# Score and PV matmuls on 128 rows instead of 64, with the low half of K stored twice

## The chip, the cores and the metric

The kernel runs on one core of one Trainium2 chip. The metric is device time in microseconds (us), the median of the runs that were timed; lower is better. The profiled execution is a single run with its own time, which is given beside its span.

## The reference

Attention over 4 batches of 8 heads (576 positions, 64 wide) feeds a maximum of three matrix products and a projection (called first and second layer here), and that feeds a routed mixture of 8 experts. Cut to what matters:

```python
q_rot, k_rot = rotate(q), rotate(k)                      # rotary embedding, (4, 8, 576, 64)
scores = (1 / np.sqrt(D)) * np.matmul(q_rot, k_rot.transpose(0, 1, 3, 2))
attn = np.exp(scores - scores.max(-1, keepdims=True))
attn = attn / (attn.sum(-1, keepdims=True) + 1e-09)
x = np.matmul(attn, v).transpose(0, 2, 1, 3).reshape(2304, 512)
h = np.maximum(np.maximum(x @ w1, x @ w2), x @ w3)       # 512 -> 768
x = h @ w_out                                            # 768 -> 512
# then: each token goes to the expert of its largest gate logit, relu(x @ w1[e]) @ w2[e]
```

## The kernel before

**Precision.** Most float32 products are made from pairs of float16: an operand is split into a high part and a low part (what the high part leaves over), and high*high, high*low and low*high are summed in PSUM. Batch 0 of the attention computes its scores in float32 instead, on 64 rows (lines 651 and 652); its PV products go the float16 way like all the others.

**Units.** The attention is a list of 36 units a batch, 144 in all, numbered from 0 through the batches: 32 units of 128 query rows by one head, and 4 tail units that hold the last 64 query rows of two heads. A unit goes through these steps, each on its own engine:

- scores on PE, in batches 1 to 3: `qt` holds Q transposed, 128 rows a head, of which 64 rows are Q's high part and 64 its low part. `kh` holds K's high part transposed and stored twice, on rows 0 to 63 and again on 64 to 127, so that one 128-row matmul gives high*high plus low*high (lines 659 and 660: 512 and 64 columns). K's low part `kl` is stored once; of two heads that share a block, one lies on rows 0 to 63 and the other on 64 to 127. Its product uses the 64 rows of `qt` with Q's high part (lines 661 and 662). Tail units do the same for two heads, each into 64 columns of the array (lines 671 to 674).
- DVE scales the scores and takes the row minimum (L677), ACT takes the exponential (L679) and its float16 high part (L681), DVE the low part (L686).
- the queue of SP transposes both into `pt` by a DMA of 9 blocks of 128 x 128 (L689).
- PV on PE: 13 matmuls on 128 rows (L713, L714, L716), and a last one on 64 rows (L717), which multiplies `pt` block 4 with the low part of V's last 64 positions.

**K and Q preparation.** Batches 1 to 3 have two halves of 4 heads each. For a half: load K and Q; a sum of squares of both gives the scales (its matmul is line 100, "the stats matmul" below); POOL and DVE apply the rotary embedding to K and then to Q (`rope_of`, lines 411 to 435; the products with the sine go into a buffer `t2`, of which there is one); ACT writes K's high part twice (L472), DVE its low part (L475, three instructions of 640, 512 and 128 elements a row); ACT and DVE split Q (L483, L486); SP transposes `khs` (18 blocks, L503), `qs` (18 blocks, L504) and `kls` (10 blocks, L505) into one tile `kq`, of which three exist. The second half of a batch is first read by the fifth unit of that batch (units 40, 76 and 112).

**Order.** Python records the instructions with priorities, and a scheduler that simulates the engines fixes each engine's order at build time. At run time every engine goes through its own list in order and waits where a semaphore tells it to. Between the units PE does first-layer (L817 to L819) and second-layer matmuls (L865 to L867) of earlier batches, which read `self.w`. The expert part begins when the attention and both layers are done, at about 660 us of the span.

## Time and profile before

| | us |
|---|---|
| median of 3 runs | 954.32 (945.73 to 957.39) |
| profiled execution, its own time | 952.98 |
| span of the profiled execution | 951.1 |
| PE busy | 830.7 (87%) |
| DVE busy | 670.7 (71%) |
| ACT busy | 574.8 (60%) |
| POOL busy | 240.5 (25%) |

The busy time of PE counts matmuls that overlap as one stretch, and a matmul's record is longer than the time until the next may start; so what a matmul costs PE is read from the starts of matmuls that follow each other. Times in the profile are counted from the start of the span.

### The profile page before, as it was taken

The page shows a single profiled execution, that of the slowest core. Times are in us where ns is not written, and L with a number is a line of the kernel's source. Part 1 is how long each engine was busy: PE and PEld are TensorE (multiplying, and loading weights), DVE is VectorE, ACT ScalarE, POOL GpSimd, SP SyncE. Part 2 cuts the span into 40 slices and gives each one's busy share as a digit, 9 for nine tenths or more (in the row PEclk, how much of TensorE's full clock was granted, in tenths as well). Part 3 has the DMA queues.
Part 4 walks back from the last instruction along what each step waited for, and adds up shares of the span by engine and source line. Part 5 has one row for each costly group of instructions (what it writes and reads, how often), then busy time and mean ns, then how long its engine had stood idle before and what let it go on. Part 6 is the DMA issues. An engine that isn't in the chain of part 4 may idle for free. (4 is left out here: it accounts for less than half of the span.)

```text
span 951.1 us, 18856 instructions
## 1 busy us (share of the span) xinstructions
PE 830.7 (87%) x7304; PEld 653.7 (69%) x7304; DVE 670.7 (71%) x1350; ACT 574.8 (60%) x1001; POOL 240.5 (25%) x232
## 2 busy tenths in 40 slices
PE   3578998779799878699989899899499999998995
PEld 2345775567576656468667577588498889997994
DVE  6997889987487787486566666534557777766771
ACT  3767888666476566475465546421545777776772
POOL 8460002421030432020030100001431644434320
PEclk9555567989799999799979999799799999999999
DMA  8698788795898897897658865720511111133110
GB/s 244 168 198 197 174 160 178 151 190 103 112 173 146 134 180 101 122 153 144 70 112 141 121 107 97 88 41 24 200 46 34 38 42 56 45 133 123 42 45 20
DMA packets 264502, 110.66 MB, mean 116 GB/s; under 512 B 240175, under 2 KB 256703, under 8 KB 263888
## 3 DMA queue, kind: packets, MB, share of 16 engines
q1 hardware_dynamic: 254848, 79.82, 48.9%
q0 software_dynamic: 9552, 29.51, 9.4%
q8 instruction: 61, 1.00, 0.6%
q14 instruction: 41, 0.34, 0.2%
HBM read 74.97 MB, written 9.80 MB: 89 GB/s over the span
## 5 line engine op out<-in xcount | busy, mean ns | idle before, releaser
L817 PE MATMUL mm<-xT,w 128*128 128x256 f16 (+1 forms) x792 | 196.8, 263 | 2.0 <-DVE h L833 0.9
L818 PE MATMUL mm<-xT,w 128*128 128x256 f16 (+1 forms) x792 | 196.6, 263 | 0.0
L819 PE MATMUL mm<-xT,w 128*128 128x256 f16 (+1 forms) x792 | 196.2, 263 | 0.0
L679 ACT ACTIVATE p<-s,bi 128x576 f32<-128x576 f32 x144 | 106.0, 736 | 96.0 <-DVE s L677 74.3
L686 DVE SCALAR_TENSOR_TENSOR p<-p,p 128x576 f16<-128x576 f32 x144 | 128.7, 899 | 15.5 <-ACT p L681 15.0
L677 DVE TENSOR_SCALAR_CACHE_REDUCE s<-s,qk_sc 128x576 f32<-128x576 f32 x108 | 88.0, 821 | 61.9 <-PE s L662 51.7
L713 PE MATMUL o<-v,pt 128*128 128x64 f16 (+1 forms) x576 | 63.4, 207 | 48.8 <-DMA pt<-p 46.5
L1127 ACT CAST h<-r 128x512 fp32r<-128x512 f32 x80 | 93.4, 1205 | 19.0 <-DMA r<-moe_w,widx 12.9
L681 ACT ACTIVATE p<-p 128x576 f16<-128x576 f32 x144 | 97.0, 680 | 4.7 <-DMA pt<-p 2.6
L1128 DVE TENSOR_TENSOR l<-r,h 128x512 fp32r<-128x512 f32 x80 | 89.8, 1162 | 5.1 <-ACT h L1127 4.6
L817 PEld LDWEIGHTS <-w 128*128 128x128 f16 x792 | 80.6, 102 | 17.2 <-issue 8.7
L819 PEld LDWEIGHTS <-w 128*128 128x128 f16 x792 | 80.8, 102 | 11.7 <-issue 4.1
L713 PEld LDWEIGHTS <-pt 128*128 128x128 f16 x576 | 48.0, 105 | 59.2 <-DMA pt<-p 51.4
L818 PEld LDWEIGHTS <-w 128*128 128x128 f16 x792 | 80.9, 102 | 10.7 <-issue 3.8
L1218 PE MATMUL pa<-xh,h 128*128 128x256 f32 x288 | 81.7, 286 | 0.8 <-ACT xh L1149 0.8
L1219 PE MATMUL pa<-xl,h 128*128 128x256 f32 x288 | 81.9, 285 | 0.2 <-DVE xl L1150 0.2
L1220 PE MATMUL pa<-xh,l 128*128 128x256 f32 x288 | 81.8, 285 | 0.0
L833 DVE SCALAR_TENSOR_TENSOR hm<-mm,winv,hm 128x512 f32<-128x512 f32 (+1 forms) x60 | 40.1, 668 | 39.3 <-PE mm L819 37.5
L651 PE MATMUL s<-kq 64*128 64x512 f32 (+1 forms) x72 | 56.9, 970 | 8.9 <-ACT p L679 8.9
L865 PE MATMUL mm<-oh,h 128*128 128x256 f16 (+1 forms) x216 | 60.4, 282 | 4.5 <-DVE hm L833 4.3
L714 PE MATMUL o<-v,pt 128*128 128x64 f16 (+1 forms) x576 | 62.7, 207 | 1.1 <-DVE v L619 1.1
L1190 PE MATMUL pb<-h,hl 128*128 128x512 f32 x152 | 60.8, 403 | 3.0 <-DVE hl L1222 2.8
(308 smaller groups left out, 2082.7 us busy)
## 6 DMA issues: line engine op xcount, KB each, us to landing
wr<-moe_w POOLq DMA_DIRECT2D x10, 768.0 KB
yscr<-y SPq DMA_DIRECT2D x18, 257.0 KB, 4.0
rk<-k SPq DMA_DIRECT2D x8, 512.0 KB, 4.3
vraw<-v SPq DMA_DIRECT2D x8, 512.0 KB, 4.6
rq<-q SPq DMA_DIRECT2D x7, 512.0 KB, 5.0
wr<-moe_w_out POOLq DMA_DIRECT2D x4, 768.0 KB
pt<-p SPq DMA_TRANSPOSE x144, 3.3
v<-v SPq DMA_DIRECT2D x16, 128.0 KB, 7.7
```

Source lines behind the costliest of these rows:

```text
L677: nc.vector.tensor_scalar(out=sf, in0=sf, scalar1=sc, scalar2=None, op0=ALU.mult, op1=ALU.min, accum_out=bi)
L679: nc.scalar.activation(p32, sf, AF.Exp, bias=bi, scale=-1.0, accum_out=st["sum", c][:, h:h + 1])
L681: nc.scalar.activation(p16[:, 0], p32, AF.Copy, scale=32768.0)
L686: nc.vector.scalar_tensor_tensor(out=p16[:, 1], in0=p32, scalar=32768.0, in1=p16[:, 0], op0=ALU.mult, op1=ALU.subtract)
L713: nc.tensor.matmul(out, lhsT=pt[:, blk], rhs=sel(vh, blk), start=blk == 0, stop=False)
L817: nc.tensor.matmul(pv[:, i], lhsT=wh, rhs=xT[:, k, :n], start=k == 0, stop=False)
L818: nc.tensor.matmul(pv[:, i], lhsT=wh, rhs=xT[:, 4 + k, :n], start=False, stop=False)
L819: nc.tensor.matmul(pv[:, i], lhsT=wl, rhs=xT[:, k, :n], start=False, stop=k == 3)
L1127: nc.scalar.copy(T["h1"][:, :, j], r[:, :, j])
L1128: nc.vector.tensor_tensor(out=T["l1"][:, :, j], in0=r[:, :, j], in1=T["h1"][:, :, j].bitcast(F32), op=ALU.subtract)
L1219: nc.tensor.matmul(ps[:, i], lhsT=h1[:, k, j + i], rhs=xl[:, k], start=False, stop=False)
L1220: nc.tensor.matmul(ps[:, i], lhsT=l1[:, k, j + i], rhs=xh[:, k], start=False, stop=k == 3)
```

## The change

In batches 1 to 3 the low part of K is laid out like the high part: all 18 blocks, stored twice (on rows 0 to 63 and on 64 to 127). The low score matmuls then take the same 128-row `qt` block as the high ones, which adds the product low*low. The last PV matmul takes all 128 rows of `pt` block 4; rows 64 to 127 of the V operand are zeros. The tail units issue their eight matmuls in another order: both heads' 512-column ones, both heads' 64-column ones, first with `kh`, then with `kl`.

What comes with it: `kls` grows from 10 to 18 blocks and takes the slot of `t2`, so the rope of Q, which needs `t2`, waits until the transposes have read `kls`; the transposes of K become a step of their own, ahead of the rope of Q. DVE makes `kls` in one instruction and POOL copies it to the second place. POOL zeroes 64 rows of each V tile. The tile `kq` grows from 48 to 54 blocks, and room for it is made by putting the tail output `xt32` into a part of `self.w` that is no longer used by then. A switch that was off (`PE_LO`) is removed with its code.

```diff
@@ split_k
-            kls = self.raws.tile([P, 10, P], F16, tag="kls", name="kls", bufs=1)
+            kls = self.raws.tile([P, 18, 2, D], F16, tag="t2", name="kls", bufs=1)
             nc.scalar.activation(khs, rot.unsqueeze(2).to_broadcast([P, 18, 2, D]), AF.Copy, scale=s)
-            for sl, d0, out in ((slice(8, 18), D, kls[:, 0:10, D:2 * D]), (slice(0, 8), 0, kls[:, 0:8, 0:D]),
-                                (slice(16, 18), 0, kls[:, 8:10, 0:D])):
-                nc.vector.scalar_tensor_tensor(out=out, in0=rot[:, sl], scalar=s, in1=khs[:, sl, 0],
-                                               op0=ALU.mult, op1=ALU.subtract)
+            nc.vector.scalar_tensor_tensor(out=kls[:, :, 0], in0=rot, scalar=s, in1=khs[:, :, 0],
+                                           op0=ALU.mult, op1=ALU.subtract)
+            nc.gpsimd.tensor_copy(kls[:, :, 1], kls[:, :, 0])
@@ tr
-            kq = self.att.tile([P, 48, P], F16, tag=f"kq{(2 * b + hf + (1 if b == 0 else -2)) % 3}", name="kq", bufs=1)
-            kh, qt, kl = kq[:, 0:18], kq[:, 18:36], kq[:, 36:46]
+        def tr_k():
+            kq = self.att.tile([P, 54, P], F16, tag=f"kq{(2 * b + hf + (1 if b == 0 else -2)) % 3}", name="kq", bufs=1)
+            kh, qt, kl = kq[:, 0:18], kq[:, 18:36], kq[:, 36:54]
             nc.sync.dma_start_transpose(out=kh, in_=st["khs"].rearrange("p a b d -> p (a b d)"))
-            nc.sync.dma_start_transpose(out=qt, in_=st["qs"].rearrange("p a d -> p (a d)"))
-            nc.sync.dma_start_transpose(out=kl, in_=st["kls"].rearrange("p a d -> p (a d)"))
+            nc.sync.dma_start_transpose(out=kl, in_=st["kls"].rearrange("p a b d -> p (a b d)"))
             self.KQ[b, hf] = (kh, kl, qt, st["sc"])
+        def tr_q():
+            nc.sync.dma_start_transpose(out=self.KQ[b, hf][2], in_=st["qs"].rearrange("p a d -> p (a d)"))
-        seq = [load, stats, self.rope_of(st, "k", b), split_k, self.rope_of(st, "q", b), split_q, tr]
+        seq = [load, stats, self.rope_of(st, "k", b), split_k, tr_k, self.rope_of(st, "q", b), split_q, tr_q]
@@ V
+                nc.gpsimd.memset(vt[64:128, 52:56], 0.0)
@@ scores, c < 4
-                nc.tensor.matmul(ps[:, 0], lhsT=qt[pr, qb], rhs=kl[pr, j * 4:j * 4 + 4], start=False, stop=True)
-                nc.tensor.matmul(ps[:, 1, :64], lhsT=qt[pr, qb], rhs=kl[pr, 8 + j, 64 * o:64 * o + 64], start=False, stop=True)
+                nc.tensor.matmul(ps[:, 0], lhsT=qt[:, qb], rhs=kl[:, hh * 4:hh * 4 + 4], start=False, stop=True)
+                nc.tensor.matmul(ps[:, 1, :64], lhsT=qt[:, qb], rhs=kl[:, 16 + j, 64 * o:64 * o + 64], start=False, stop=True)
@@ scores, tail
-                for o in range(2):
-                    ...
+                for first, kk in ((True, kh), (False, kl)):
+                    for tail in range(2):
+                        for o in range(2):
+                            ...
+                            nc.tensor.matmul(out, lhsT=qt[:, 16 + j, pr], rhs=rhs, start=first, stop=not first)
@@ PV
-            nc.tensor.matmul(out, lhsT=pt[0:64, 4], rhs=last(), start=False, stop=True)
+            nc.tensor.matmul(out, lhsT=pt[:, 4], rhs=last(), start=False, stop=True)
@@ constants
-PRE_AT, PRE_N = 2, 7
+PRE_AT, PRE_N = 2, 8
```

The scheduler makes a new order for every engine. On the queue of SP, at the second half of batch 3, the three transposes into `kq` stand before as follows (L689 is the `pt` of a unit, L790 the input of the first layer):

```order
L689 DMA_TRANSPOSE pt<-p_6633 128x9x128
L503 DMA_TRANSPOSE kq<-khs 128x18x128
L505 DMA_TRANSPOSE kq<-kls 128x10x128
L689 DMA_TRANSPOSE pt<-p_6681 128x9x128
L790 DMA_TRANSPOSE xT<-x_6657 128x8x128
L504 DMA_TRANSPOSE kq<-qs 128x18x128
L689 DMA_TRANSPOSE pt<-p_6875 128x9x128
```

and after the change (lines of the changed file: L671 is `pt`, L772 the input of the first layer, L485, L486 and L490 the three transposes):

```order
L485 DMA_TRANSPOSE kq<-khs 128x18x128
L671 DMA_TRANSPOSE pt<-p_6600 128x9x128
L671 DMA_TRANSPOSE pt<-p_6632 128x9x128
L486 DMA_TRANSPOSE kq<-kls 128x18x128
L772 DMA_TRANSPOSE xT<-x_6656 128x8x128
L671 DMA_TRANSPOSE pt<-p_6680 128x9x128
L671 DMA_TRANSPOSE pt<-p_6873 128x9x128
L671 DMA_TRANSPOSE pt<-p_6910 128x9x128
L671 DMA_TRANSPOSE pt<-p_6952 128x9x128
L671 DMA_TRANSPOSE pt<-p_6966 128x9x128
L490 DMA_TRANSPOSE kq<-qs 128x18x128
```

Q's transpose moved from the place behind the `pt` of unit 107 to the place behind that of unit 111, directly ahead of the first unit that reads it. On POOL, in the same half, the ropes of K and Q, with the routing's copies (L940) and index writes (L945) between them, stand before as

```order
L422 TENSOR_TENSOR t_5991<-rk,rope 128x16x32 x2
L424 TENSOR_TENSOR t_5991<-rk,rope 128x2x32 x2
L432 TENSOR_TENSOR rk<-rk,t_5991 128x1152
L940 COPY y<-cst 128x1 x3
L945 DMA islot<-rows,pi 18432x1 x2
L422 TENSOR_TENSOR t_6215<-rq,rope 128x16x32 x2
L945 DMA islot<-rows,pi 18432x1
L424 TENSOR_TENSOR t_6215<-rq,rope 128x2x32 x2
L432 TENSOR_TENSOR rq<-rq,t_6215 128x1152
```

and after (L405, L407 and L415 are the rope, L922 and L927 the routing, L458 the copy of `kls`)

```order
L415 TENSOR_TENSOR rk<-rk,t_5991 128x1152
L922 COPY y<-cst 128x1
L927 DMA islot<-rows,pi 18432x1
L922 COPY y<-cst 128x1
L927 DMA islot<-rows,pi 18432x1 x2
L458 COPY kls<-kls 128x18x64
L405 TENSOR_TENSOR t_6217<-rq,rope 128x16x32
L407 TENSOR_TENSOR t_6217<-rq,rope 128x2x32
L405 TENSOR_TENSOR t_6217<-rq,rope 128x16x32
L407 TENSOR_TENSOR t_6217<-rq,rope 128x2x32
L415 TENSOR_TENSOR rq<-rq,t_6217 128x1152
```

The copy of `kls` stands behind the routing's entries, and Q's rope behind the copy. On PE the order around the same place changes too: between the stats matmul of that half and the first score of unit 112 stand 128 first- and second-layer matmuls, 6 units' scores and 6 PV products before, and 197, 8 and 11 after. For unit 40 the layer matmuls are 216 before and 269 after, with 6 and 10 PV products; for unit 76 they are 105 and 242, with 4 and 15 units' scores and 7 and 15 PV products. Behind the last PV product of the attention stand 51 first-layer matmuls fewer than before.

## Rows read from the trace of the kernel before

**Rows 1.** Busy time by stage (engines, clock of PE, DMA share, GB/s).
```profile
60.00:180.00 120.00, 105.30 (x775) 74.09 (x775) 106.75 (x223) 92.88 (x178) 19.48 (x21) 0.65 0.85 184
180.00:630.00 450.00, 403.39 (x4306) 300.25 (x4304) 310.55 (x723) 259.50 (x529) 75.61 (x68) 0.93 0.78 125
630.00:660.00 30.00, 29.83 (x280) 26.47 (x279) 13.04 (x61) 5.89 (x12) 2.14 (x3) 1.00 0.10 27
```

**Rows 2.** What PE waited for, 180 to 630 us: total, times, longest.
```profile
PE o L713 <- DMA pt<-p: 38.4, 16, 6.5
```

**Rows 3.** Timeline of PE around 411 us: start, duration, instruction, rows*columns.
```profile
410.87 0.19 PE L660 MATMUL s<-kq 128*128 128x64 f16 x1
410.99 0.39 PE L661 MATMUL s<-kq 64*128 64x512 f16 x1
411.22 0.19 PE L662 MATMUL s<-kq 64*128 64x64 f16 x1
411.34 0.28 PE L819 MATMUL mm<-xT,w 128*128 128x256 f16 x1
411.46 0.27 PE L817 MATMUL mm<-xT,w 128*128 128x256 f16 x1
...
412.68 0.31 PE L716 MATMUL o<-v,pt 128*128 128x64 f16 x5
412.92 0.20 PE L717 MATMUL o<-v,pt 64*128 64x64 f16 x1
413.05 0.28 PE L817 MATMUL mm<-xT,w 128*128 128x256 f16 x1
```

**Rows 4.** Groups by line and shape: count, busy time, mean ns.
```profile
L661 PE MATMUL s<-kq 64*128 64x512 f16 x96 | 38.1, 397 | 0.0
...
L717 PEld LDWEIGHTS <-pt 64*128 64x128 f16 x144 | 13.6, 94 | 9.4
```

**Rows 5.** Timeline of PE in a tail unit.
```profile
304.99 0.19 PE L672 MATMUL s<-kq 128*64 128x64 f16 x1
305.11 0.40 PE L673 MATMUL s<-kq 64*64 64x512 f16 x1
305.35 0.19 PE L674 MATMUL s<-kq 64*64 64x64 f16 x1
305.47 0.40 PE L671 MATMUL s<-kq 128*64 128x512 f16 x1
```

**Rows 6.** Timelines of DVE and POOL around 326 to 335 us.
```profile
327.10 2.52 DVE L686 SCALAR_TENSOR_TENSOR p<-p,p 128x576 f16<-128x576 f32 x1
...
334.57 0.75 DVE L686 SCALAR_TENSOR_TENSOR p<-p,p 128x576 f16<-128x576 f32 x1
...
326.00 3.00 POOL L432 TENSOR_TENSOR rq<-rq,t 128x1152 f32<-128x1152 f32 x1 [2.29 <-DVE rq L428]
```

**Rows 7.** Batch 3, second half: timelines of POOL, ACT, SP, PE; L504's landing.
```profile
477.20 2.48 POOL L422 TENSOR_TENSOR t<-rq,rope 128x512 f32<-128x512 f32 x2 [11.06 <-DMA rq<-q]
...
483.49 3.01 POOL L432 TENSOR_TENSOR rq<-rq,t 128x1152 f32<-128x1152 f32 x1 [0.70 <-DVE rq L428]
488.27 2.21 ACT L472 ACTIVATE khs<-rk,sc_qks 128x2304 f16<-128x2304 f32 x1
490.51 2.71 SPq L503 DMA_TRANSPOSE kq<-khs  x1
493.77 1.33 SPq L505 DMA_TRANSPOSE kq<-kls  x1
500.25 2.91 SPq L504 DMA_TRANSPOSE kq<-qs  x1
DMA to landing us min/median/max: 6.4/6.4/6.4
507.14 0.38 PE L659 MATMUL s<-kq 128*128 128x512 f16 x1
```

**Rows 8.** What POOL waited for, 180 to 630 us: total, times, longest.
```profile
POOL islot L945 <- DVE pi L935: 60.0, 3, 49.2
```

More of the change, by code (lines that the diff above doesn't have):

```diff
@@ L148, in load_consts @@
         nc.sync.dma_start(self.tri, self.A["tri"])
-        self.neg16 = self.const.tile([P, P], F16, name="neg16")
-        nc.gpsimd.tensor_scalar(out=self.neg16, in0=self.ident, scalar1=-1.0, scalar2=None, op0=ALU.mult)
         nc.gpsimd.tensor_scalar(out=self.cum[:, 0], in0=self.cst[:, C_IOTA8:C_IOTA8 + 8], scalar1=float(NT // P), scalar2=None,
@@ L336, in go @@
                 nc.scalar.activation(h, c, AF.Copy, scale=s)
-                if w not in PE_LO:
-                    nc.vector.scalar_tensor_tensor(out=l, in0=c, scalar=s, in1=h, op0=ALU.mult, op1=ALU.subtract)
-                    return
-                for i in range(2):
-                    po = self.mm.tile([P, 512], F32, tag="mm", name="wlo")[:, :384]
-                    if w < 3:
-                        ci, hi, li = (t[:, 384 * i:384 * i + 384] for t in (c, h, l))
-                    else:
-                        ci, hi, li = (t[:, 3 * i:3 * i + 3] for t in (c, h, l))
-                        po = po.rearrange("p (f a) -> p f a", f=3)
-                    nc.tensor.matmul(po, lhsT=st["eye", w], rhs=ci, start=True, stop=False)
-                    nc.tensor.matmul(po, lhsT=self.neg16, rhs=hi, start=False, stop=True)
-                    LO_EV(nc, li, po, w, i)
+                nc.vector.scalar_tensor_tensor(out=l, in0=c, scalar=s, in1=h, op0=ALU.mult, op1=ALU.subtract)
             return go
@@ L665, in s_part @@
                 kh, kl, qt, sc = self.KQ[b, hf]
-                for o in range(2):
-                    pr = slice(64 * o, 64 * o + 64)
-                    hh = 2 * o + j
-                    q = qt[:, 16 + j, pr]
-                    ql = qt[pr, 16 + j, pr]
-                    nc.tensor.matmul(ps[pr, 0], lhsT=q, rhs=kh[:, hh * 4:hh * 4 + 4], start=True, stop=False)
-                    nc.tensor.matmul(ps[pr, 1, :64], lhsT=q, rhs=kh[:, 16 + j, pr], start=True, stop=False)
-                    nc.tensor.matmul(ps[pr, 0], lhsT=ql, rhs=kl[pr, j * 4:j * 4 + 4], start=False, stop=True)
-                    nc.tensor.matmul(ps[pr, 1, :64], lhsT=ql, rhs=kl[pr, 8 + j, pr], start=False, stop=True)
+                for first, kk in ((True, kh), (False, kl)):
+                    for tail in range(2):
+                        for o in range(2):
+                            pr = slice(64 * o, 64 * o + 64)
+                            hh = 2 * o + j
+                            out, rhs = (ps[pr, 1, :64], kk[:, 16 + j, pr]) if tail else (ps[pr, 0], kk[:, hh * 4:hh * 4 + 4])
+                            nc.tensor.matmul(out, lhsT=qt[:, 16 + j, pr], rhs=rhs, start=first, stop=not first)
             sf = ps.rearrange("p a b -> p (a b)")[:, 0:S]
```

13 lines of the change are left out of this document (3 added, 10 removed).

## The prediction

> **What bounds the kernel now.** I read the busy time by stage first. Between 180 and 630 us, where batches 1 to 3 of the attention run with both layers between their units, PE is busy for 403.4 of 450 us, DVE for 310.6, ACT for 259.5, POOL for 75.6, and the DMA engines have a share of 0.78. From 630 to 660 us the attention is over and PE alone works off layer matmuls, 29.8 of 30 us [rows 1]. So no chain of the attention sets the start of the expert part; the sum of PE's work does, and PE's waits. The view of waits says what PE's idle time is: 38.4 us in 16 places before a PV product whose `pt` has not landed [rows 2]. Everything else that PE waits for in the stretch is far smaller. Hence the frame of the sum: a microsecond less of work on PE in this stretch is a microsecond less in the end, unless a wait for `pt` grows by it.
>
> Then I read how PE's matmuls follow each other [rows 3]. A 64-column matmul of the same shape as the one before it costs PE 0.03 us: the five L716 last 0.31 us together and one lasts 0.19, so four steps take 0.12. But from L660 (64 columns, 128 rows) to L661 (64 rows) 0.12 us pass, and from L662 (64 columns, 64 rows) to the next 128-row matmul again 0.12. At the end of a PV product the fifth L716 starts at 412.68 + 0.12 = 412.80, L717 at 412.92, and the matmul behind L717 at 413.05: 0.12 and 0.13 where 0.03 is the rule. So each change between 64 and 128 rows costs about 0.09 us, 0.10 behind L717, in which PE neither computes nor waits for anything that a semaphore shows.
>
> **The change part by part.**
>
> *The pauses that go.* There are 96 units with 128 query rows in batches 1 to 3 [rows 4], each with two changes of the row count around L661 and L662: 96 x 2 x 0.09 = 17.3 us. There are 144 L717 [rows 4], one a unit with both sides: 108 of them in batches 1 to 3, 108 x (0.09 + 0.10) = 20.5 us. A tail unit has the change twice, once for each head: 0.12 us from L672 to L673 and from L674 to the second L671 [rows 5]; in the new order the row count never changes and three of the four pauses go (the one in which PE comes back from 64 columns to the layers stays): 12 x 3 x 0.09 = 3.2 us. Together 41.0 us of PE's time in the stretch that PE bounds. The number of matmuls and their columns stay; that 128 rows cost no more than 64 is seen in L659 and L661 in the trace, whose 512 columns take 0.38 and 0.39 us [rows 3, 7].
>
> The other 36 L717 are batch 0's, 36 x 0.19 = 6.8 us. There DVE is busy for 106.8 of 120 us, PE for 105.3, at a granted clock of 0.65 [rows 1]: two engines that nearly bound it together. I count half, 3.4 us, and keep 0 and 6.8 for the range.
>
> *What the waits for `pt` take back.* The order of PE is fixed, and a PV product stands a few units behind its scores. Three units' scores and PV products between them become shorter by 3 x (0.18 + 0.19) = 1.1 us, while the way over DVE, ACT, DVE and the DMA stays as long. Where PE waits already, that 1.1 us comes back as more waiting: 16 x 1.1 = 17.8 us [rows 2]. That is the upper bound for the waits that exist; the lower one is nothing, if the new order puts enough layer matmuls ahead of those places. I take half, 9 us.
>
> *DMA.* `kls` has 18 blocks instead of 10. SP's queue is held for 1.33 us by the 10 blocks and 2.71 us by 18 [rows 7], so 6 x 1.38 = 8.3 us more over the whole attention, and as much for the DMA engines. At a share of 0.78, which becomes 0.78 x 450 / 420 plus 8.3 / 420 = 0.86, this makes some `pt` later, but not the chain as a whole. 0 to 8.3; I take 1.
>
> *POOL and DVE.* The copy of `kls` is not in the trace. Its nearest row is POOL's add of the same number of elements, 3.0 us [rows 6], from two float32 inputs; the copy reads one float16 input, so 3.0 is its upper bound, and I use it. Six copies make 18 us of POOL, which is busy for 75.6 of 450 us [rows 1]: hidden, but not free for DVE. The same L686 takes 0.75 us alone and 2.52 us where it starts inside POOL's add, and it ends together with the add [rows 6]. If each copy holds up DVE for its whole length it is 18 us of DVE, which has 139 us of idle time there; what reaches PE is a late `pt`, and I let at most half of it through. 0 to 9; I take 1. The Trainium skill says the same of the mechanism in "SBUF — State Buffer", section "Who interferes with whom": a DVE instruction with two SBUF inputs and a GpSimd instruction that reads SBUF exclude each other for their whole length. By that rule, which speaks against putting the copy on POOL, every copy can cost DVE its full length, 9 us in the sum; by the row an operation of POOL did so once, and the sum keeps its 1. The memsets of V (eight, one operand of 256 elements on 64 rows) write only and lie ahead of V's conversion, and DVE gets one `kls` instruction for three: both at nothing.
>
> *K and Q.* This is the step that moves. In the second half of batch 3, Q's rope started on POOL at 477.2 us, before K's high part was scaled at 488.27, and ended at 486.5; Q's transpose was issued at 500.25 and landed 6.4 us later, at 506.7; the first score that reads it started at 507.14 [rows 7]. So before, Q arrives half a microsecond ahead of its use. Now Q's rope must stand behind the copy (3.0), the transposes of K (6.4 to landing) and then take its own 486.5 - 477.2 = 9.3 us. K's high part is written until 490.5, its low part needs some 1.5 us more (an estimate: the L686 above does half the elements in 0.75), so K's landing is at 490.5 + 1.5 + 3.0 + 6.4 = 501.4 and Q's rope ends at 510.7 at the latest. From there to the transpose, the splitting of Q took anything from 3 us to the 9.8 us between 490.5 and 500.25. Q is then late by 13 to 20 us. Against that, PE's order has been given more to do between the stats matmul and the first score that needs Q: 69 layer matmuls of 0.12 us (411.34 to 411.46 [rows 3]), two units' scores and five PV products of some 0.45 us, 11.4 us in all. At unit 40 it is 53 matmuls and 4 PV products, 8.2 us, at unit 76 25 us. What is left is at most 20 - 11.4 = 9 us at unit 112 and 12 us at unit 40, nothing at unit 76, and at the least 2 and 5. But these matmuls are work that PE has to do anyway, and a missing Q delays scores first; PE itself stops only when it reaches them. 0 to 21; I take 3. Of the queues that Q's transpose is moved past, SP's holds the `pt` of the next unit behind it, which cannot exist before Q has landed.
>
> The sum is -41.0 - 3.4 + 9 + 1 + 1 + 3 = -30.4 us. The profiled execution took 952.98 us (a span of 951.1), which becomes 922.6; the median of the runs is 1.3 us above it, so the forecast is 924 us.
>
> **The rivals.** *The waits take it back.* If every wait deepens (17.8), DMA and DVE cost their bounds (8.3 and 9) and batch 0 gives nothing, the sum is -41.0 + 35.1 = -6 us and the time 948; what lies from there down to the edge of the forecast, 936, is this case too. For it: a fixed order, and a DMA share of 0.78 that rises. Against it: PE waits in 16 places for 108 PV products, so most have room.
>
> *The pause belongs to something else*, to matmuls with K in general, say, and not to the row count. Then nothing is gained, and the added work costs some 5 us: 959. Against it: from L661 to L662, both with K and both on 64 rows, 0.23 us pass for 512 columns, which is eight of the 0.03 us steps of 64 columns and leaves no pause; and L717 has nothing to do with K.
>
> *Q comes too late.* POOL's copy stands behind the routing's index writes, which have waited up to 49.2 us for their indices [rows 8], and the whole way of Q stands behind the copy. Where PE arrives at units 40, 76 and 112 with its layer matmuls used up, it stops until Q has landed. At 20 us in each of the three batches, without any layer matmul to cover it, that is 60 us in place of the 3 that I took: 981. It makes the change a loss from 33 / 3 = 11 us a batch, and one that a measurement can tell (19 us) from 17 us a batch. For it: the half microsecond to spare before. Against it: the extra matmuls ahead of units 40, 76 and 112.
>
> *Tail units overlap.* In the new order the two heads' matmuls, on different columns of the array, stand next to each other. If two run at once, a tail unit saves two further steps of 0.24 us (L673 to L674 [rows 5]): 12 x 0.48 = 5.8 us, 918, and with no wait deepened 905. No row shows two at once; before, they never stood next to each other without a change of rows. By the Trainium skill, "TensorEngine Tiling (Array Packing)", section "Key Properties", tiles work independently and can run matmuls in parallel; by that rule the tail units gain this, by the rows the sum stands as it is.
>
> **How the numbers follow.** A measurement of this kernel tells about 2% from no change, 19 us: faster ends at 935, slower begins at 973. Chances: the forecast, between 905 and 935, 0.60; still better, with tail overlap or fewer waits than before, 0.10; the waits take it back, 0.17; the pause belongs to something else, 0.05; Q too late by so much that it is slower, 0.08. Faster 0.70, same 0.22, slower 0.08. The range goes down to -41.0 - 6.8 - 5.8 = -54 us from 954, about 900, with a little for waits that the new order removes: 898. Up, it takes in the waits' case to 950. What lies outside is the rest of the better case and the last two.
>
> **What would show it right or wrong.** In the changed profile the steps into and out of the low score matmuls and the last PV matmul should be 0.03 us where they were 0.12 and 0.13. PE's busy time between 180 us and the end of the layers should be some 40 us less; the wait of L713's successor for `pt` should lie between 40 and 60 us. Copies of `kls` should take up to 3.0 us. At units 40 and 112 the first score should start right after Q's landing, with PE busy on layer matmuls until then; if PE stands idle there for more than some 3 us together, the K and Q term is too small. If the steps are gone and the time is not, the waits have taken it. The prediction would be wrong at its root if those steps stayed at 0.12.

## The result and the profile after

The changed kernel took 930.98 us (median of four runs, 928.8 to 933.53), the kernel before, run beside it, 953.67 us (945.73 to 957.39). The ratio is 0.9759, with a 95% interval of 0.9723 to 0.9796: 22.7 us faster, where the prediction said 30. The profiled execution took 929.0 us, with a span of 927.2 us.

By stage, the view that answers to [rows 1] (columns: window, its length, busy time of PE, PEld, DVE, ACT and POOL, PE's granted clock, the share of the DMA engines, GB/s):

```profile
60.00:180.00 120.00, 103.89 (x889) 77.75 (x886) 108.26 (x226) 94.66 (x179) 22.81 (x24) 0.67 0.85 177
180.00:630.00 450.00, 381.12 (x4449) 306.90 (x4450) 319.78 (x766) 262.52 (x537) 86.94 (x84) 0.94 0.83 131
630.00:660.00 30.00, 17.44 (x125) 14.37 (x124) 12.87 (x17) 13.01 (x16) 9.08 (x11) 0.77 0.42 158
```

From 180 to 630 us PE gets through 4449 matmuls where it did 4306, in 22 us less busy time, and the layers end inside the last window, in which PE was busy throughout before. The share of the DMA engines rises from 0.78 to 0.83.

The line numbers fall by 15 to 18: the score matmuls are now L643 to L646 (a tail unit's are L656), the PV product is L695 to L699, and the layers are L799 to L801 and L847 to L849. The timeline of PE around 411 us answers to [rows 3] (start, duration, instruction, rows*columns, and in brackets the idle time ahead of it with what ended it):

```profile
409.14 0.19 PE L644 MATMUL s<-kq 128*128 128x64 f16 x1
409.17 0.38 PE L645 MATMUL s<-kq 128*128 128x512 f16 x1
409.39 0.19 PE L646 MATMUL s<-kq 128*128 128x64 f16 x1
411.30 0.20 PE L695 MATMUL o<-v,pt 128*128 128x64 f16 x1 [1.72 <-DMA pt<-p]
...
411.54 0.31 PE L698 MATMUL o<-v,pt 128*128 128x64 f16 x5
411.68 0.19 PE L699 MATMUL o<-v,pt 128*128 128x64 f16 x1
411.71 0.27 PE L849 MATMUL mm<-oh,h 128*128 128x256 f16 x1
```

The steps are gone. From L644 to L645 it is 0.03 us (0.12 before), out of L699 it is 0.03 (0.13 before); the fifth L698 starts at 411.54 + 0.12 = 411.66, so the step into L699 is 0.02 to 0.03 as well. (The step out of L646 can't be read here, because a wait follows.) But in the same rows PE stands for 1.72 us ahead of this PV product.

A tail unit is one row now, where [rows 5] had a step between each pair. A whole one before, from its first row to the layer matmul behind it, and one after:

```profile
319.15 0.40 PE L671 MATMUL s<-kq 128*64 128x512 f16 x1
...
320.60 0.28 PE L817 MATMUL mm<-xT,w 128*128 128x256 f16 x1
```

```profile
320.79 0.68 PE L656 MATMUL s<-kq 128*64 128x512 f16 x8
321.40 0.28 PE L801 MATMUL mm<-xT,w 128*128 128x256 f16 x1
```

Eight matmuls, four of 512 columns and four of 64, cost PE 0.61 us up to the start of the next matmul, where they cost 1.45. One behind the other without pauses they would need 4 x 0.22 + 4 x 0.03 = 1.0 us (the steps of L643 to L646 at the same clock), so the two heads run at the same time.

What PE waited for between 160 and 620 us (total, times, longest), to be held against [rows 2]:

```profile
PE o L695 <- DMA pt<-p: 56.5, 40, 6.0
PE s L643 <- ACT p L661: 5.6, 6, 2.2
```

Waits for `pt` went from 38.4 us in 16 places to 56.5 us in 40 (the first line reads the same from 180 to 630 us, the window of [rows 2]).

For this kernel and every one below I added up two things over the same piece of the program, from the first matmul to the first transposition of the expert part: the idle times ahead of PE's matmuls that are longer than 0.15 us (waits), and what is left of the stretch (work, the pauses in it). Before, the expert part began at 675.1 us, with 92.5 us of waits and 572.9 us of work; after, at 649.1 us, with 116.0 and 522.9. So PE's work shrank by 50.0 us and its waits grew by 23.5. The expert part itself takes 2.1 us longer (951.1 - 675.1 = 276.0 and 927.2 - 649.1 = 278.1 us to the span's end).

These sums come from one profiled execution of each kernel, and the work in them depends on TensorE's granted clock, which has two levels here: a step between two layer matmuls of 256 columns takes 0.109 us at the upper level (2.4 GHz) and 0.213 us at the lower (1.2 GHz). Counted from the first score of batch 1 on, the kernel before did 50.2 us of its work at the lower level and the changed kernel 49.2 us, so the clock has no part in their difference there. In some runs below it has.

### The profile page after: what moved, and what is told of

Its sections match the earlier page's. It is cut to its first block, busy times and chain, and to the rows that moved or that the text cites. A ratio compares the mean times of both kernels' runs of the same rounds, so it can differ in the third digit from the quotient of the medians.

```text
span 927.2 us, 18852 instructions
## 1 busy us (share of the span) xinstructions
PE 782.3 (84%) x7304; PEld 641.5 (69%) x7304; DVE 670.2 (72%) x1338; ACT 574.5 (62%) x1001; POOL 249.5 (27%) x245
## 4 chain that ended last, share of the span: by engine, by line
PE 36%; DMA 15%; issue 4%; DVE 4%; ACT 2%; POOL 2%; SPq 0%; POOLq 0%; ACTq 0%; DVEq 0%
DMA pt<-p 7%; DMA out<-o,di 5%; PE mm L800 4%; PE mm L799 4%; PE mm L801 4%; PE pa L1201 3%; PE pa L1200 3%; PE pa L1202 3%; PE pb L1172 3%; PE pb L1170 3%; PE pb L1171 3%; PE mm L847 1%; PE mm L849 1%; DMA kq<-kls 1%; PE mm L848 1%
## 5 line engine op out<-in xcount | busy, mean ns | idle before, releaser
L799 PE MATMUL mm<-xT,w 128*128 128x256 f16 (+1 forms) x792 | 195.7, 262 | 3.1 <-DVE hm L815 2.6
L801 PE MATMUL mm<-xT,w 128*128 128x256 f16 (+1 forms) x792 | 195.0, 261 | 0.0
L668 DVE SCALAR_TENSOR_TENSOR p<-p,p 128x576 f16<-128x576 f32 x144 | 121.5, 846 | 26.8 <-ACT p L663 26.5
L695 PE MATMUL o<-v,pt 128*128 128x64 f16 (+1 forms) x576 | 63.0, 208 | 68.9 <-DMA pt<-p 64.8
L695 PEld LDWEIGHTS <-pt 128*128 128x128 f16 x576 | 47.7, 106 | 84.0 <-DMA pt<-p 76.7
L799 PEld LDWEIGHTS <-w 128*128 128x128 f16 x792 | 80.9, 102 | 13.3 <-DVE hm L815 2.0
L801 PEld LDWEIGHTS <-w 128*128 128x128 f16 x792 | 80.7, 102 | 8.8 <-issue 0.7
L847 PE MATMUL mm<-oh,h 128*128 128x256 f16 (+1 forms) x216 | 61.8, 288 | 4.8 <-DVE hm L815 3.4
L1170 PE MATMUL pb<-h,hh 128*128 128x512 f32 x152 | 61.6, 408 | 0.9 <-ACT hh L1203 0.9
L927 POOL DMA_INDIRECT islot<-rows,pi x18 | 19.2, 1069 | 159.1 <-DVE pi L917 93.3
```

The costliest lines, as they stand in the source:

```text
L668: nc.vector.scalar_tensor_tensor(out=p16[:, 1], in0=p32, scalar=32768.0, in1=p16[:, 0], op0=ALU.mult, op1=ALU.subtract)
L695: nc.tensor.matmul(out, lhsT=pt[:, blk], rhs=sel(vh, blk), start=blk == 0, stop=False)
L799: nc.tensor.matmul(pv[:, i], lhsT=wh, rhs=xT[:, k, :n], start=k == 0, stop=False)
L801: nc.tensor.matmul(pv[:, i], lhsT=wl, rhs=xT[:, k, :n], start=False, stop=k == 3)
```

## The experiments

All ratios are to the kernel before, each run beside it on the same chip. Theory A says that the pauses belong to a change of the number of rows. Of the waits that grew by 23.5 us, theory B says that PE ran ahead of work whose pace it doesn't set; theory C that they come from what the change adds beside PE, namely the second copy of `kls`, its additional DMA blocks and the later Q. Theory D is C's narrower form, Q alone. Theory E came with the runs: that the scheduler's order, which any edit moves, is worth as much as the edit.

### The two halves of the change

The last PV matmul back on 64 rows; the order of the instructions on every engine stays that of the changed kernel:

```diff
-            nc.tensor.matmul(out, lhsT=pt[:, 4], rhs=last(), start=False, stop=True)
+            nc.tensor.matmul(out, lhsT=pt[0:64, 4], rhs=last()[0:64], start=False, stop=True)
```

> The changed kernel with one edit undone: the last PV matmul of each unit reads 64 rows again; every engine's order of instructions stays that of the changed kernel. Theory A (the pauses belong to a change of the number of rows): the step into that matmul and the one out of it go from 0.03 back to about 0.12 us, 144 units x 0.19 = 27 us of PE time. What the time does with it tells two theories of the waits apart. Theory B (TensorE's waits grew from 92.5 to 116.0 us because it ran ahead of work whose pace it doesn't set): waits shrink by about half of the 27 us, the time is about 944 us (ratio to the kernel before 0.990). Theory C (the waits grew by what the change added beside TensorE: the second copy of K, the additional DMA blocks, a later Q): they stay as they are, about 956 us (ratio 1.004). Rival to A (the pause belongs to the tile or to the accumulation's end): steps stay at 0.03 and the ratio at 0.976.

Measured: 942.27 us, ratio 0.9842 (0.9792 to 0.9892), where B said 0.990 and C 1.004. The profiled execution took 934.87 us. The timeline of PE at the same PV product as above, and its waits:

```profile
411.22 0.19 PE L646 MATMUL s<-kq 128*128 128x64 f16 x1
412.65 0.20 PE L695 MATMUL o<-v,pt 128*128 128x64 f16 x1 [1.24 <-DMA pt<-p]
...
412.89 0.31 PE L698 MATMUL o<-v,pt 128*128 128x64 f16 x5
413.14 0.20 PE L699 MATMUL o<-v,pt 64*128 64x64 f16 x1
413.27 0.28 PE L849 MATMUL mm<-oh,h 128*128 128x256 f16 x1
```

```profile
PE o L695 <- DMA pt<-p: 48.0, 28, 5.6
```

With 64 rows in one matmul alone, 0.13 us are back on both of its sides (412.89 + 0.12 to 413.14, and on to 413.27): theory A, with no other edit and no other order. And the wait ahead of this very product is 1.24 us where it was 1.72. Over the whole, work is 546.4 us (23.5 more than in the changed kernel), waits 101.5 us (14.5 less). At the same order, 62% of what the PV pauses cost came back as waiting. That is theory B. Theory C, by which the waits stay at 116, falls.

The two parts of the stretch differ. Up to the first score of batch 1, which starts at 182.6 us here and at 183.8 in the changed kernel, the changed kernel has 6.8 us less of work and 7.3 us more of waits: batch 0 gains nothing. From there on it is 16.7 us less of work and 7.3 us more of waits, 44%.

The low score matmuls of the regular units back on 64 rows, PV at 128:

```diff
-                nc.tensor.matmul(ps[:, 0], lhsT=qt[:, qb], rhs=kl[:, hh * 4:hh * 4 + 4], start=False, stop=True)
-                nc.tensor.matmul(ps[:, 1, :64], lhsT=qt[:, qb], rhs=kl[:, 16 + j, 64 * o:64 * o + 64], start=False, stop=True)
+                pr = slice(64 * o, 64 * o + 64)
+                nc.tensor.matmul(ps[:, 0], lhsT=qt[pr, qb], rhs=kl[pr, hh * 4:hh * 4 + 4], start=False, stop=True)
+                nc.tensor.matmul(ps[:, 1, :64], lhsT=qt[pr, qb], rhs=kl[pr, 16 + j, 64 * o:64 * o + 64], start=False, stop=True)
```

> The changed kernel with the other half undone: the low score matmuls of the regular units read 64 rows again (rows 0 to 63 or 64 to 127 of the doubled K), the PV matmuls stay at 128 rows, K is still doubled and Q still roped late. Theory A: 96 units x 2 steps go from 0.03 to 0.12, 17 us of PE time. With theory B about half shows: ratio 0.985; with theory C all of it: 0.994. If the two halves simply add up, this ratio and that of the run without the PV half lie together as far above 0.976 as 1 lies, about.

Measured: 943.85 us, ratio 0.9834 (0.9777 to 0.9891), near B's 0.985; C's 0.994 lies outside. Work 550.6 us, waits 106.8. The order is another one than the changed kernel's, so this one is read against the next, which has the same order on PE.

Both undone, by both edits above:

> The changed kernel with both halves undone: low score matmuls of the regular units and the last PV matmuls read 64 rows again; K is still doubled (its second copy and the additional DMA blocks are there), Q is still roped late, and the tail units keep 128 rows. What is left is the price of what the change added, less the tail units' gain of some 3 to 9 us. Theory B (waits grew because TensorE ran ahead): the added parts cost the 5 us forecast, ratio 0.995 to 1.003. Theory C (the added parts made the waits): 20 us or more of waits stay, ratio above 1.010.

Measured: 958.82 us, ratio 0.9991 (0.9927 to 1.0055). Work 571.4 us, waits 94.0, which is the kernel before to within 1.5 us each (572.9 and 92.5). Its waits for `pt`, and those of the kernel before, both from 160 to 620 us:

```profile
PE o L696 <- DMA pt<-p: 37.6, 21, 6.2
```

```profile
PE o L713 <- DMA pt<-p: 40.5, 19, 6.5
```

Here the copy, the additional blocks and the late Q are all in place, and the waits for `pt` are no longer than before; theory C is out a second time. But the ratio isn't the bare price of what the change adds beside PE, because the tail units keep their gain in this run: PE's time in them is 9.2 us, 20.8 before. That the work comes out equal all the same is the clock's doing: from the first score of batch 1 on, 70.5 us of work were done at the lower level, 50.2 before, which is some 10 us by the steps above (an estimate). So the added parts can cost as much as the tail units gain, 11.7 us at most, with the ratio's 6 us either way; the waits show none of it. The pair with the run above, which shares its order on PE, gives the PV half a second price: work down by 20.8 us, waits up by 12.8, again 62%; from the first score of batch 1 on 21.7 and 10.2, 47%. Batch 1 starts at 181.7 us here and at 185.3 in the run above.

The PV half alone, made from the kernel before (V's tail rows set to zero, the last PV matmul on 128 rows):

```diff
+                nc.gpsimd.memset(vt[64:128, 52:56], 0.0)
-            nc.tensor.matmul(out, lhsT=pt[0:64, 4], rhs=last(), start=False, stop=True)
+            nc.tensor.matmul(out, lhsT=pt[:, 4], rhs=last(), start=False, stop=True)
```

> The kernel before with the PV half alone: V's tail rows are set to zero and the last PV matmul reads 128 rows; K is not doubled, Q is roped where it was, scores are as before. Pauses of 144 x 0.19 = 27 us go. Theory B: something over half of it is taken back as waits, ratio 0.984 to 0.991. Theory C: all of it shows, ratio 0.972. Beside the run with the low scores on 64 rows (0.983, K doubled, Q late), the difference of the two is the price of K's and Q's part, 5 us forecast, less the tail units.

Measured: 947.88 us, ratio 0.9883 (0.9814 to 0.9952). Work 553.1 us (19.8 less than before), waits 104.5 (12.0 more, 61%). It falls into B's range. PE's order is that of the kernel before; from the first score of batch 1 on (181.1 us before, 182.1 here) work is 18.4 us less and waits 9.4 more, 51%. The two halves, 0.0117 for this one and 0.0158 for the one that keeps the 128-row scores, add up to 0.0275 where both together gave 0.0241, the same within the intervals.

### Parts beside PE

Q's rope with a scratch buffer of its own (`qs`, which is free then), so that it needn't wait for K's transposes:

```diff
-            t2 = self.raws.tile([P, 18, D], F32, tag="t2", name="t2", bufs=1)
+            if nm == "q":
+                t2 = st["qs"].rearrange("p a d -> p (a d)").bitcast(F32).rearrange("p (a d) -> p a d", d=D)
+            else:
+                t2 = self.raws.tile([P, 18, D], F32, tag="t2", name="t2", bufs=1)
```

> The changed kernel, with the scratch of Q's rope laid into a buffer that is free at that time, so that Q's rope no longer waits for K's scratch and Q's transposes are issued earlier (before the scores of about unit 25, 55 and 91 in place of 30, 53 and 91 of the first halves, and earlier in DMA order by up to 5 units). Theory D (the waits grew because Q is late at units 40, 76 and 112): waits of TensorE fall by 10 to 20 us, ratio 0.956 to 0.966. Theory B (TensorE runs ahead of the rest everywhere): waits stay within 4 us of 116, ratio 0.972 to 0.980.

Measured: the times were 952.93, 961.77, 1817.89 and 3047.73 us; the last two can't be explained, and no ratio is formed. In the profiled execution (961.77 us) waits are 143.0 us, 27 more than in the changed kernel. Theory D, by which they fall by 10 to 20 us, got no support. The run is a poor test of it: the order moved too (see below), and Q's transposition came earlier for unit 40 alone (issued at 195.9 us, in the changed kernel at 213.8), and later for unit 112 (502.8 and 498.7). What decides against D is the changed kernel's own view of waits from 160 to 620 us, in which PE and its weight loads wait for Q's transposition once:

```profile
PEld L643 <- DMA kq<-qs: 0.2, 1, 0.2
```

The tail units' matmuls head by head:

```diff
-                for first, kk in ((True, kh), (False, kl)):
-                    for tail in range(2):
-                        for o in range(2):
+                for o in range(2):
+                    for first, kk in ((True, kh), (False, kl)):
+                        for tail in range(2):
```

> The changed kernel with the tail units' six matmuls issued head by head (one head's three, then the other's), not alternately; same rows, same columns. In the changed kernel the two heads' matmuls start 3 to 4 ns apart. If that overlap is worth what the rows say, the tail units take some 5.8 us of PE time more, and half of it shows: ratio 0.979; if all, 0.982. If the overlap is hidden behind waits: 0.976. The order elsewhere differs a little from unit 104 on, worth 2 us either way as an estimate.

Measured: 936.41 us, ratio 0.9781 (0.9732 to 0.983). (The edit orders eight matmuls a unit; the six in the expectation is a slip.) Work is 528.4 us, 5.5 more than in the changed kernel, and waits are the same, 115.9. That is near the 5.8 us expected, but it isn't the overlap: 4.7 of the 5.5 us lie ahead of the first score of batch 1, where the edit changes nothing. And the overlap is still there. A whole tail unit, and one whose last two matmuls stand behind a PV product:

```profile
322.46 0.69 PE L656 MATMUL s<-kq 128*64 128x512 f16 x8
323.09 0.28 PE L801 MATMUL mm<-xT,w 128*128 128x256 f16 x1
```

```profile
319.12 0.68 PE L656 MATMUL s<-kq 128*64 128x512 f16 x6
...
320.25 0.43 PE L656 MATMUL s<-kq 128*64 128x512 f16 x2
```

Eight matmuls cost 0.63 us here and 0.61 in the changed kernel. That the order on PE is head by head shows in the second unit: the two matmuls left over are one of 512 and one of 64 columns (0.36 us up to the next), the end of one head, where the changed kernel's alternating order leaves two of 64. The run doesn't price the overlap, then, because it doesn't undo it; it shows that the overlap doesn't hang on the order of issue. Its price is read from the tail units before and after, below. In time, the difference to 0.9759 is inside the intervals.

The second copy of `kls` on ScalarE:

```diff
-            nc.gpsimd.tensor_copy(kls[:, :, 1], kls[:, :, 0])
+            nc.scalar.copy(kls[:, :, 1], kls[:, :, 0])
```

> The changed kernel with the second copy of K's low half on ScalarE in place of GpSimd (12 copies of some 1 to 2 us; ScalarE is 58% busy there). If the copy on GpSimd, which shares VectorE's memory path in the rows, costs anything by delaying GpSimd's own work or VectorE's softmax: 1 to 5 us less, ratio 0.971 to 0.975; if nothing hangs on it: 0.976; if ScalarE's copies push the exponentials back: up to 0.982.

Measured: 939.95 us, ratio 0.9805 (0.9746 to 0.9865). (There are 6 copies, not 12.) Waits 119.1 us. Taking the copy off GpSimd brings nothing that this run can tell: its interval holds all three cases of the expectation, and the order moved too.

### What sets the waits

One unit more between scores and PV product (with a buffer taken from the half-precision weights for the space):

```diff
-LAG = 3
+LAG = 4
-P16, PT = 4, 3
+P16, PT = 3, 4
```

> The changed kernel with one unit more between a unit's scores and its PV matmuls (4 in place of 3; for the space one buffer of the half-precision weights less, one more of the transposed ones). TensorE's waits for the transposed weights are 56.5 us, 40 times. If they are the time that one unit's chain (softmax, conversion, DMA transposition) takes, a longer distance hides most: ratio 0.940 to 0.960. If the engines or the DMA queues before them have no room (a rate, not a delay), or the buffer taken away binds: 0.970 to 0.985.

Measured: 950.36 us, ratio 0.9899 (0.9843 to 0.9956). And the taken buffer alone:

```diff
-P16, PT = 4, 3
+P16, PT = 3, 3
```

> The changed kernel with 3 in place of 4 buffers of the half-precision weights, distance still 3: the part of the run with distance 4 that was given up for space. If that buffer is what made the longer distance slower: ratio 0.985 to 0.995. If the longer distance itself (scores issued earlier push other work back): 0.974 to 0.980.

Measured: 944.93 us, ratio 0.9882 (0.9801 to 0.9964). PE's waits for `pt` between 160 and 620 us, first with distance 4, then with the buffer taken alone:

```profile
PE o L695 <- DMA pt<-p: 65.9, 41, 7.5
```

```profile
PE o L695 <- DMA pt<-p: 68.5, 39, 9.6
```

Both are above the changed kernel's 56.5. The longer distance has not hidden them, but it can't be told from the lost buffer, which alone gives the same time, nor from another order alone (see below).

Six of the nine blocks of each unit's weights transposed (left out are the low parts of the weights from column 192 on; their matmuls read another block):

```diff
-            nc.sync.dma_start_transpose(out=pt, in_=p16.rearrange("p a b -> p (a b)"))
+            nc.sync.dma_start_transpose(out=pt[:, 0:6], in_=p16.rearrange("p a b -> p (a b)")[:, 0:768])
-                nc.tensor.matmul(out, lhsT=pt[:, 4 + blk], rhs=sel(v2, blk), start=False, stop=False)
+                nc.tensor.matmul(out, lhsT=pt[:, 4 + min(blk, 1)], rhs=sel(v2, blk), start=False, stop=False)
```

> The changed kernel with 6 of the 9 blocks of each unit's weights transposed by DMA (left out: the low parts of the weights from column 192 on; their PV matmuls run as before on block 5). TensorE's, VectorE's and ScalarE's instructions keep their number and size; of DMA work between 180 and 600 us, which is at 0.83 to 0.92 in the changed kernel, a good fifth goes. Theory B1 (what TensorE ran ahead of is the DMA's transposition): its waits for the transposed weights fall from 56.5 to under 35 us, ratio 0.945 to 0.960. Theory B2 (it ran ahead of VectorE's and ScalarE's softmax): they fall only by the shorter landing, about 40 x 0.5 = 20 us at most of waits or less, ratio 0.965 to 0.976.

Measured: 942.79 us, ratio 0.9868 (0.9782 to 0.9954). The stage, the wait, and the DMA queue with the median time to landing (180 to 600 us):

```profile
180.00:630.00 450.00, 371.88 (x4367) 300.44 (x4367) 312.40 (x722) 261.02 (x534) 86.43 (x83) 0.93 0.67 107
```

```profile
PE o L695 <- DMA pt<-p: 63.2, 29, 6.3
```

```profile
pt<-p SPq DMA_TRANSPOSE x111, 3.2
```

and in the changed kernel, by the same view:

```profile
pt<-p SPq DMA_TRANSPOSE x113, 3.9
```

The share of the DMA engines falls from 0.83 to 0.67, a transposition lands 0.7 us sooner, and PE waits no less: 63.2 us for `pt`, in 29 places for 40, and 125.6 in all. So B1's range is missed. That the rate of the DMA transposition has no part in the waits isn't shown by it, since PE's order is another one too.

The same, with VectorE's low parts on 192 of 576 columns:

```diff
-            nc.vector.scalar_tensor_tensor(out=p16[:, 1], in0=p32, scalar=32768.0, in1=p16[:, 0],
+            nc.vector.scalar_tensor_tensor(out=p16[:, 1, 0:192], in0=p32[:, 0:192], scalar=32768.0, in1=p16[:, 0, 0:192],
```

> As the run with 6 of 9 blocks, and VectorE computes the low parts of the weights for 192 of 576 columns (the others aren't used there), some 0.4 us less in each of 144 units. B1: no more than 3 us under the run with 6 blocks alone. B2: clearly under it, by 10 us or more, since VectorE is on the way to every transposition.

Measured: 944.89 us, ratio 0.9864 (0.9784 to 0.9944). VectorE's instruction (busy time, mean ns, idle time ahead) and the wait:

```profile
L668 DVE SCALAR_TENSOR_TENSOR p<-p,p 128x192 f16<-128x192 f32 x144 | 61.2, 428 | 21.9 <-ACT p L663 21.0
```

```profile
PE o L695 <- DMA pt<-p: 71.7, 35, 6.7
```

L668 takes 0.43 us instead of 0.85 (121.5 us busy in the changed kernel, 61.2 here), and the time stays. B1 and B2 both miss their ranges; here, too, the order is another one than in the run before.

Another order alone, by moving one number of the schedule:

```diff
-MOE_SHIFT = 22
+MOE_SHIFT = 21.9
```

> The changed kernel with one number of the schedule moved (MOE_SHIFT 21.9 in place of 22), so that the steps of the mixture layers stand a little elsewhere; nothing else changes. It shows what another order alone is worth. Theory E (the size of the gain hangs on the order that the scheduler happens to find): more than 6 us from the changed kernel, ratio under 0.969 or over 0.982. Else 0.972 to 0.980.

Measured: 950.46 us, ratio 0.9909 (0.9867 to 0.9951), ten runs. The profiled execution (953.22 us): waits of PE from 160 to 620 us, and the stage:

```profile
PE o L695 <- DMA pt<-p: 55.9, 39, 5.9
PE mm L799 <- ACT hm L813: 8.8, 3, 6.5
PE ps_sc L100 <- ACT qs L436: 8.5, 3, 4.7
```

```profile
180.00:630.00 450.00, 366.55 (x4227) 291.30 (x4226) 307.37 (x710) 256.57 (x522) 85.38 (x81) 0.91 0.81 130
```

Theory E holds, and more strongly than I had thought. The same instructions in a slightly different order are 1.5% slower, and the interval doesn't touch the changed kernel's. PE's waits are 130.5 us in place of 116.0; the waits for `pt` are the same, and others have come: a layer's first matmul waits for its activation (L799), a stats matmul for K's squares (L100). The granted clock from 180 to 630 us is 0.91 in place of 0.94, and the work takes 533.5 us in place of 522.9. Most of these 10.6 us are the clock's: from the first score of batch 1 on the work is 10.3 us longer, and 66.7 us of it were done at the lower level, 49.2 in the changed kernel; 17.5 us more at steps of 0.213 in place of 0.109 us are 8.5 us. No version ran faster than the changed kernel.

The six kernels that have all the changed matmuls at 128 rows and leave no computation out, by ratio (the run with Q's scratch is left out):

```
changed kernel            0.9759
tail units by heads       0.9781
copy on ScalarE           0.9805
one buffer less           0.9882
distance 4                0.9899
MOE_SHIFT 21.9            0.9909
```

All are faster than the kernel before, and the changed kernel lies at the good end. No other order of the kernel before was run, so where that one lies among its own orders is not known.

## Why the prediction was right, and what it had wrong

**The frame.** A microsecond less of PE's work was to be a microsecond less in the end, unless a wait for `pt` grew by it. The "unless" turned out to be the main thing: of 50.0 us of work, 26.0 reached the start of the expert part. The forecast of 30 for 22.7 us came from two terms that were both too small and in part cancel: 44.4 us of work for 50.0, and 14 us of returns for 23.5.

**The pauses.** Right, in mechanism and size. The steps into the low score matmul and the last PV matmul and out of the latter went from 0.12 or 0.13 to 0.03, and those of the PV matmul came back in the run that undid it alone. PE's work is 50.0 us less; the prediction had 41.0 + 3.4 and, with all of batch 0, 47.8, and the tail units gave more than the 3.2 us in it (next point). Batch 0's pauses, which I counted at half, show no gain: in each of the three pairs with one order on PE, the first score of batch 1 starts 1.0 to 3.6 us later without the PV pauses than with them.

**The rival of the tail units** came true as a mechanism: a whole tail unit went from 1.45 to 0.61 us at the upper clock, 10 us for twelve, where the prediction's two terms were 3.2 for the pauses and 5.8 for the overlap. The Trainium skill's rule in "TensorEngine Tiling (Array Packing)", section "Key Properties", that tiles can run matmuls in parallel, agrees with that row. The rival had the cause half right: the heads now stand next to each other, but the run with head-by-head order overlaps as well, so what had kept them apart before was the change of rows between them. The time that I gave to it, 918, didn't come, because of the next point.

**What the waits for `pt` take back.** This is the term that was mis-sized. I set it at 9 us, with an upper bound of 17.8 from the 16 places in which PE waited already. The waits for `pt` grew by 18.1 us, twice the term, and from 16 places to 40; all waits of PE together grew by 23.5. The upper bound was passed, if only just, because it was made from one kind of waits alone: it let existing ones deepen and had no room for new ones. In the three pairs with one order on PE, place by place and from the first score of batch 1 on, existing waits for `pt` grew by 4.4, 4.4 and 4.7 us (about 0.2 to 0.3 us each, where the PV half of the bound is 0.57), and new ones came at 11.5, 8.1 and 7.0 us while 7.9, 1.9 and 3.6 us of old ones went. Over the whole stretch the waits took back 61 to 62% of the PV half; from the first score of batch 1 on 44 to 51%, and ahead of it nothing of the gain was left. Over the whole change it was 23.5 / 50.0 = 47%. With 23.5 in place of the 14 us that all the added and returned terms made, and 50.0 in place of 44.4, the sum is -26.5, near the measured -24.0 of the two profiled executions; the 2.1 us longer expert part is most of the rest.

**DMA, POOL, DVE.** Together 2 us in the sum. No run isolates them: with the PV and score pauses back, the ratio is 0.9991, and that holds the tail units' gain. The copy of `kls` and its neighbours in the changed kernel (count, shortest, median and longest ns, first and last start):

```profile
L456 DVE SCALAR_TENSOR_TENSOR kls<-rk,sc_qks,khs x6: 1407/1415/1419, 134.6 to 474.2; 128x1152 f16<-128x1152 f32 x6
L458 POOL COPY kls<-kls x6: 1145/1606/2019, 136.1 to 475.7; 128x1152 f16<-128x1152 f16 x6
L486 SPq DMA_TRANSPOSE kq<-kls x6: 2806/2938/3424, 141.6 to 479.5; - x6
```

The copy takes 1.15 to 2.02 us, under the bound of 3.0; SP's queue is held for 2.9 us by 18 blocks, as I had it (2.71). What the copy does to DVE can be read directly, in a copy on POOL and the L668 on DVE that starts inside it:

```profile
315.52 1.15 POOL L458 COPY kls<-kls 128x1152 f16<-128x1152 f16 x1 [19.58 <-DVE kls L456]
316.19 1.09 DVE L668 SCALAR_TENSOR_TENSOR p<-p,p 128x576 f16<-128x576 f32 x1 [0.73 <-ACT p L663]
```

L668 ends 0.61 us behind the copy's end (316.67), and so do the three others that start well inside one; alone it takes 0.75 us. So it stands until the copy is through and then runs. In [rows 6] it is the same, and I misread it: that L686 ends at 329.62, not together with the add but 0.62 us behind it. The rule of the Trainium skill in "SBUF — State Buffer", section "Who interferes with whom", that the two exclude each other, agrees with these rows. The full price that the prediction gave it, 18 us of DVE and 9 in the sum, doesn't come, because only four L668 in six copies start so: they take 1.04 to 1.70 us, some 2 us too much in all.

**K and Q.** Right. In the second half of batch 3, POOL (timeline; idle time ahead in brackets) and Q's transpose (by tile) show the chain that I worked out:

```profile
475.68 1.61 POOL L458 COPY kls<-kls 128x1152 f16<-128x1152 f16 x1 [11.22 <-DVE kls L456]
486.19 1.27 POOL L405 TENSOR_TENSOR t<-rq,rope 128x512 f32<-128x512 f32 x1 [8.90 <-DMA kq<-kls]
...
491.33 2.62 POOL L415 TENSOR_TENSOR rq<-rq,t 128x1152 f32<-128x1152 f32 x1 [2.10 <-DVE rq L411]
```

```profile
L490 SPq DMA_TRANSPOSE kq<-qs x1: 2816/2816/2816, 498.7 to 498.7; - x1
DMA to landing us min/median/max: 4.8/4.8/4.8
```

Q lands at 498.7 + 4.8 = 503.5 us, and the first score that reads it starts at 504.9, the unit's before it at 484.7: 20 us without scores. In them PE works on layers and PV products and stands for 3.0 us only, none of it for Q. At unit 40 Q is the last to come, as the prediction expected: its transposition is issued at 213.8 us and lands 5.5 us later, at 219.3, where its first score starts. But PE has layers and PV products to do there, too, and Q costs it the 0.2 us wait of the weight load shown above. So the 3 us of the term are nearer to nothing, and the rival by which Q comes too late is out: the copy stood behind the routing's entries, yet what POOL waited for was DVE (11.22 us, first row), and the layers covered Q's delay.

**What no step had** is the order. I took the order that the scheduler found as given, with terms of a few microseconds on it. Other orders of the same work end up to 14 us later by the ratios (0.9909 - 0.9759 = 0.0150 of 954 us). Of the 22.7 us gained, a part may therefore be luck of the order, or the tuning of its numbers to it; how large it is stays open, since the kernel before was run in one order only. The parts that are shown at a fixed order on PE are the PV half's: 0.0083 (changed kernel against the one with PV on 64 rows; their intervals just touch), 0.0157 (the pair with scores on 64 rows) and 0.0117 (the PV half alone against the kernel before).

**What stays open** is what PE ran ahead of, in detail. Neither less DMA transposition nor shorter low parts on VectorE, nor a longer distance between scores and PV, made the waits smaller; but each of these runs had another order, worth as much as the effect that was looked for, so none of them rules its cause out. A run in which one engine's work shrinks while every engine's order stays would settle it; it wasn't tried.

## What to carry to other kernels

A matmul on another number of rows than its neighbours cost 0.09 to 0.10 us at each change, with nothing in the view of waits to show it; look for it as a step longer than the columns explain, and fill the rows with zeros or doubled data where that is cheap beside PE. Then count on the waits: on an engine with a fixed order that waits for others already, about half of the time saved came back as waiting where that engine set the pace, in new places too, and no gain was left where a second engine was as busy (batch 0). A bound made from the existing waits alone leaves out a part. Read the clock before two sums of work are compared: one run here had 10 us more of the same work, 8.5 of them by steps at the lower level. And before a difference of one or two per cent is put down to an edit, move a number of the schedule that has nothing to do with it, and see what another order is worth.

## What was not expected of the hardware

- Two heads' matmuls on different columns of the array ran at once without being told to: eight matmuls in 0.61 us, where one behind the other they need 1.0. Issued head by head they still did, in 0.63 us; changes of the number of rows between them, as in the kernel before, kept them apart, 1.45 us with the pauses.
- An instruction of DVE with two inputs in SBUF (L668) that starts inside POOL's copy ends 0.61 us behind the copy, whatever the copy's length.
- Taking a third of the blocks out of every transposition of the weights lowered the share of the DMA engines from 0.83 to 0.67 and the median time to landing from 3.9 to 3.2 us only, and PE's waits were no shorter, at another order of its matmuls.
- The order that differs by a tenth in one number cost PE 14.5 us of waits and, at a granted clock of 0.91 in place of 0.94 between 180 and 630 us, 10.6 us of work for the same matmuls, most of it by steps at the lower level of the clock.
